# A 2:4 sparse linear layer on one core: SyncE loads x tile 5, tile 6 is transposed second, eight instead of fourteen short fillers, and other hand-written orders

## The chip, the core and the metric

The kernel runs on one core of one Trainium2 chip. The metric is the device time of one execution in microseconds, the median of several runs. TensorE is called PE in the profile, its weight loads PEld, VectorE DVE, ScalarE ACT, GpSimd POOL, SyncE SP.

## What is computed

```
wg  = w.reshape(256, 4, 1024)              # groups of four rows of w
mag = abs(wg)
thr = second largest of the four magnitudes
wp  = (wg * (mag >= thr)).reshape(1024, 1024)
out = einsum("bsd,df->bsf", x, wp) + b     # x: 16 x 512 x 1024, bf16
```

Each column of each group of four weights keeps its two largest. The pruned matrix then multiplies 8192 rows of x (64 tiles of 128 tokens), and the bias is added.

## The kernel before, in words

All 64 token tiles need 1024x1024 pruned weights, which don't exist at the start. The kernel therefore prunes the weights in six pieces (`pieces`, L137) and lets TensorE start on the first seven token tiles while later pieces are still being pruned. Pieces 0 to 3 are 256 columns each of the upper 512 rows, pieces 4 and 5 are 512 columns each of the lower 512 rows. A weight row of four neighbours lies on one partition ("packed"), so x must be transposed with the same grouping.

The start runs as follows. Loads: SyncE and ScalarE each issue half of weight piece 0 (L124, L125); then ScalarE issues x tile 5 and x tile 6 (L126, L127; upper half of the columns, 128 KB each), and SyncE tiles 3 and 4 together (L129, 256 KB), weight piece 1, tile 2, tiles 0 and 1, pieces 2, 3 and 4, and a transposing load of whole tiles (`load_lead`, L118). TensorE meanwhile runs fillers (L410, L411), matmuls of ones: six of 512 columns and fourteen of 128. After them four lists of tokens, written out by hand, set the order of each engine (L275 to L297); `run` (L400) emits them so that every token's forerunners (`needs`, L313) have been emitted, and the tile framework adds the semaphores. A list is the program order of its engine. The tokens are:

- `T5a`: TensorE transposes x tile 5 in four 128x128 steps (L203) into a PSUM bank; `C5a`: ScalarE copies it to SBUF (L208). Tiles in `LOOSE` (L196) use a bank of the larger PSUM pool, the others one of two banks, and then wait for the copy two transposes before.
- `abs hi lo t1 t2 thr mask mult` with a piece number: VectorE's pruning of that piece (L177, L166). For piece 0, `g` and `h` are rows 2 and 3 of each group in columns 0-127 and 128-255, `u` and `v` are rows 0 and 1 over all 256 columns; `x` and `y` are rows 0-1 and 2-3 of another piece. A token `abs3` in ScalarE's list is done by ScalarE (L169).
- `M5.0g`: TensorE's partial product of tile 5 with part g of piece 0 (L237). The partial products of pieces 0 to 3 for tiles 0 to 6 add up in PSUM banks (`psum_o`, six banks in rotation); `S3b0`, `U6h0`: ScalarE copies a full bank to SBUF (`stage`, L273), which frees it.
- `W0.0` and so on: SyncE (once ScalarE) re-spreads pruned weights into the natural row layout (`spread`, four DMAs); `Z`: loads of piece 5 and the bias; `X1`, `Y1`, `Y0`: transposing loads of x.
- `E`, `A`: first halves of later tiles in the natural layout (L251).

Behind the lists come the closes (second halves of tiles 0 to 11) and then seven batches of x tiles that TensorE multiplies with the full weights, 16 matmuls of 512 columns a tile. VectorE adds the bias and ScalarE issues the stores.

Of the kernel before, what the change touches and what calls it, by code (L numbers as in the profile page):

```python
# [10 lines left out]
def kernel(  # L11
# [62 lines left out]
    def pe(i):  # L74
        return seq("pe", i)
# [19 lines left out]
    def tokens(dram, t):  # L95
        a, b_ = next(s for s in GROUPS if s[0] <= t < s[1])
        return dram[a * P:b_ * P].rearrange("(p t) k -> p t k", p=P), t - a
    bias_sb = const.tile([P, Dout], bf16)

    def issue(eng, out_, in_):  # L100
        q = nc.sync if eng == "sp" else nc.scalar
        return seq(eng, q.dma_start(out_, in_))

    def load_w(g, c0, c1, ma=0, mb=4, eng="sp"):
        issue(eng, w_sb[:, g, ma:mb, c0:c1], wv[:, g, ma:mb, c0:c1])

    def load_x(ta, tb, eng="sp"):
        xs = const.tile([P, tb - ta, HK], bf16, name=f"x_{ta}")
        xv, n = tokens(xf, ta)
        issue(eng, xs[:], xv[:, n:n + tb - ta, :HK])  # L110
        for t in range(ta, tb):
            x_sb[t] = xs[:, t - ta, :]
# [10 lines left out]

    load_w(0, 0, 256, 0, 2)  # L124
    load_w(0, 0, 256, 2, 4, "act")  # L125
    load_x(5, 6, "act")  # L126
    load_x(SOLO, SOLO + 1, "act")  # L127
    act(nc.scalar.activation(spark[:], nc.const_aps.tensor(1.0, [P, 1], bf16), Act.Abs))
    load_x(3, 5)  # L129
# [13 lines left out]
    def filler(n, rep=1):  # L143
        for _ in range(n):
            pe(nc.tensor.matmul(warm_ps[:, :rep * P], lhsT=nc.const_aps.tensor(1.0, [P, P], bf16),  # L145
                                rhs=nc.const_aps.tensor(1.0, [P, rep * P], bf16), start=True, stop=True))
# [46 lines left out]
                self.tt(wp[:, self.g, ms, self.c0 + ca:self.c0 + cb], self.w[:, ms, ca:cb], self.mag[:, ms, ca:cb], Alu.mult)  # L193

    xpk = {}
    LOOSE = (4, 6)  # L196

    def transpose(t):
        xg = x_sb[t].rearrange("p (q m) -> p m q", m=4)
        bank = psum_o.tile([P, FH], fp32, name="ps") if t in LOOSE else psum_t.tile([P, FH], fp32, name="tp")  # L200
        tp = bank[:].bitcast(bf16)[:, :FH].rearrange("p (m q) -> p m q", m=4)
        for m in range(4):
            pe(nc.tensor.transpose(tp[:, m, :], xg[:, m, :], ident[:]))  # L203
        xpk[t] = tp
# [4 lines left out]
        xpk[t] = xt  # L209

    ps_open = {}
    SPLIT = {0: 6}
    part = {"": slice(0, 4), "x": slice(0, 2), "y": slice(2, 4), "a": slice(0, 2), "b": slice(2, 4)}
    part.update({c: slice(m, m + 1) for m, c in enumerate("uvst")})
    part.update({c: slice(2, 4) for c in "gh"})
    cols = {"g": (0, 128), "h": (128, 256), "j": (0, 128), "k": (128, 256)}
    half = {"a": slice(0, 1), "b": slice(1, 2)}
    pairs = [(3, 4), (SOLO, NPK), (0, 1), (2, 5)]
    pair_of = {t: q for q, pr in enumerate(pairs) for t in pr}
# [2 lines left out]
    def mm_piece(t, i, ms, cut=None):  # L222
# [8 lines left out]
        if new:  # L231
            ps_open[key] = psum_o.tile([P, FH], fp32, name="ps")
            left[key] = sum(SPLIT.get(a, 4) for a in ((0, 1) if t == SOLO and c0 < FH else (2, 3) if t == SOLO else (n, n)))
        ps = ps_open[key]
# [33 lines left out]
    def stage(key):  # L268
        solo = key[1] == "h"
        q, h, at = (pair_of[key[0]], key[2], int(key[0] != SOLO)) if solo else (key[0], key[1] // 2, key[1] % 2)  # L270
        if (q, h) not in staged:
# [2 lines left out]

    order = {  # L275
# [7 lines left out]
        ),  # L283
        "dve": (
# [4 lines left out]
        ),  # L289
        "act": (  # L290
            "C5a C3a C4a C6a C2a C0a C1a S3b0 S2b0 abs3 S0b0 U6h0 S3b1 S0b1 S2b1 S3b2 S0b2 S2b2 S2b3 S0b3 U6h1 "
            "S3b3 U7h0 W1.0q U7h1"
        ),
        "sp": (
            "W0.0 Z W0.1 X1 W1.0p Y1 W1.1 Y0"
# [1 line left out]
    }  # L297
    written = {"X0"}
    p = {}
    halves = {0: tuple("ghuv"), 1: ('x', 'y'), 2: ('u', 'v', 'y'), 3: ('x', 'y')}  # L300

    by_rows = {0}

    def all_of(tok, i):
        return [tok + x for x in halves.get(i, ("",))]

    def split_tok(tok):
        k = tok[-1] if tok[-1] in "xyabuvstghjk" else ""
        return (tok[:-1] if k else tok), k

    transposed = []

    def needs(eng, tok):  # L313
        base, k = split_tok(tok)
        if tok[0] == "C":
            return ["T" + tok[1:]]
        if tok[0] == "T":
            return ["C" + transposed[-2]] if int(tok[1:-1]) not in LOOSE and len(transposed) > 1 else []
        if tok[0] == "F":
            return []  # L320
        if tok[0] == "W":
            g, h = map(int, tok[1:4].split("."))
            return [n for i, pc in enumerate(pieces) if pc[0] == g and pc[1] // FH == h for n in all_of(f"mult{i}", i)]
        if tok[0] in "XYZ":
            return ["A0h1"] if tok == "Y1" else []
        if tok[0] == "A":
            return ["X0", f"W0.{tok.split('h')[1]}"] + ([f"U{NPK}h{tok[-1]}"] if tok[1] == "3" else [])
        if tok[0] == "E":
            return ["X0", f"W0.{tok[1]}"]
        if tok[0] == "U":  # L330
            t, h = map(int, tok[1:].split("h"))
            if t == NPK:
                return [f"E{h}"]
            return [f"M{t}.{x}" for i, pc in enumerate(pieces) if pc[0] == 0 and pc[1] // FH == h for x in all_of(str(i), i)]
        if base[0] == "M":
            t, i = base[1:].split(".")
            return [f"C{t}a", f"mult{i}{k}"]
        if tok[0] == "S":
            q, n = map(int, tok[1:].split("b"))
            return [f"M{t}.{x}" for i, pc in enumerate(pieces) if pc[0] == 0 and pc[1] // CW == n  # L340
                    for t in pairs[q] for x in all_of(str(i), i)]
        i, step = base[-1], base[:-1]
        before = {"abs": [], "hi": ["abs"], "lo": ["abs"], "t1": ["hi"], "t2": ["lo"],
                  "thr": ["t1", "t2"], "mask": ["thr", "hi", "lo"], "mult": ["mask"]}[step]
        out_ = []
        for b_ in before:
            if b_ in ("t1", "thr") and int(i) in SPLIT:
                out_ += [b_ + i + s for s in {"j": "j", "k": "k", "g": "j", "h": "k"}.get(k, "jk")]
            elif b_ == "t2":
                out_.append(b_ + i)  # L350
            elif b_ in ("abs", "hi", "lo") and int(i) in by_rows:
                out_ += [b_ + i + k] if step in ("hi", "lo") else [b_ + i + s for s in "ab"]
            else:
                out_.append(b_ + i + (k if b_ == "mask" else ""))
        return out_

    def emit(eng, tok):
        base, k = split_tok(tok)
        if tok[0] == "T":
            transpose(int(tok[1:-1]))  # L360
            if int(tok[1:-1]) not in LOOSE:
                transposed.append(tok[1:])
# [37 lines left out]
    def run(queues):  # L400
        while any(queues.values()):
            moved = False
            for eng, toks in queues.items():
                while toks and all(n in written for n in needs(eng, toks[0])):
                    emit(eng, toks[0])
                    written.add(toks.pop(0))
                    moved = True
            assert moved, queues

    filler(6, 4)  # L410
    filler(14)  # L411
    run({eng: order[eng].split() for eng in order})

    def load_nat(ta, tb):
# [120 lines left out]
```

## Time and profile before

| | us |
|---|---|
| median of 3 runs (232.63 to 233.07) | 232.82 |
| the profiled execution, its own time | 232.65 |
| its span, first to last instruction | 230.9 |
| PE busy | 227.4 |
| DVE busy | 107.8 |
| ACT busy | 13.3 |
| first filler starts | 0.78 |
| first transpose starts | 4.82 |
| first partial product starts | 6.07 |
| first matmul in the natural layout (E0) starts | 19.08 |

PE's busy time is modelled from pipelined matmuls: one of 128 columns is shown as 219 ns at full pace although the next one starts 56 ns later, so starts or the chain's rows tell the pace. In the timeline `x8` means eight instructions in one row, the first number is the start of the first, the second their busy time. A DMA's row has the time in which its engine issued it; when the data has landed is told by the rows of the issues.

### The profile page before, as it was taken

Reading aid. Unit: us, or ns where it says so; the run is one execution under the profiler, and the core shown is the slowest. Engines: PE = TensorE matmul, PEld = TensorE weight load, DVE = VectorE, ACT = ScalarE, POOL = GpSimd, SP = SyncE. Lnnn points to the kernel's source line nnn. Section 1 sums busy time; section 2 is a strip of 40 time slices with the busy share of each in tenths; the row PEclk is TensorE's granted clock in tenths of the full one; section 3 lists DMA queues with packets and bytes.
Section 4 is the critical chain, followed back from the end, with each engine's and each line's share of the span. In section 5 each row is a group of like instructions: output and inputs, shape, how many; then the busy total and the mean of one; then the engine's idle time right before and its main releaser. Section 6 shows DMA issues by size and latency. Waiting matters only on the chain.

```text
span 230.9 us, 2858 instructions
## 1 busy us (share of the span) xinstructions
PE 227.4 (99%) x1158; PEld 111.3 (48%) x1158; DVE 107.8 (47%) x196; ACT 13.3 (6%) x26; POOL 17.6 (8%) x15
## 2 busy tenths in 40 slices
PE   8999999999999999999999999999999999999995
PEld 5985444444444444444444444444444444444443
DVE  4999787744424424424424423423423433433434
ACT  3665100000000000000000000000000000000000
POOL 1000299700000000000000000000000000000000
PEclk9999999999999999999999999999999999999999
DMA  6999989995899322991159622796129932122122
GB/s 207 305 221 224 192 180 245 246 278 147 310 222 258 114 91 73 242 276 72 67 105 282 204 94 76 162 252 182 60 91 195 281 115 89 50 91 91 54 85 91
DMA packets 79292, 38.19 MB, mean 165 GB/s; under 512 B 64176, under 2 KB 71728, under 8 KB 79280
## 3 DMA queue, kind: packets, MB, share of 16 engines
q1 hardware_dynamic: 68352, 20.75, 44.9%
q10 hardware_dynamic: 10928, 17.27, 21.5%
q8 instruction: 9, 0.15, 0.3%
q14 instruction: 3, 0.02, 0.0%
HBM read 3.28 MB, written 16.78 MB: 87 GB/s over the span
## 4 chain that ended last, share of the span: by engine, by line
PE 99%; DVE 0%; issue 0%
PE ps L251 88%; PE ps L237 5%; PE tp L251 2%; PE ps L145 2%; PE tp L203 1%; PE ps L203 0%; DVE o L443 0%
## 5 line engine op out<-in xcount | busy, mean ns | idle before, releaser
L251 PE MATMUL ps<-wp_nat,xb 128*128 128x512 bf16 (+2 forms) x848 | 179.8, 375 | 0.0
L251 PEld LDWEIGHTS <-xb 128*128 128x128 bf16 x848 | 82.4, 98 | 97.5
L443 DVE TENSOR_TENSOR o<-ps,bias_sb 128x512 bf16<-128x512 f32 (+1 forms) x112 | 71.6, 677 | 113.8 <-PE ps L251 113.7
L439 POOL TENSOR_TENSOR st<-st,bias_sb 128x1024 f32<-128x1024 f32 x8 | 16.8, 2142 | 0.0
L251 PE MATMUL ps<-wp_nat,xlead 128*128 128x512 bf16 x64 | 14.8, 379 | 0.0
L251 PEld LDWEIGHTS <-xlead 128*128 128x128 bf16 x88 | 8.6, 98 | 10.2
L237 PE MATMUL ps<-wp,xt 128*128 128x256 bf16 (+1 forms) x126 | 13.0, 261 | 0.0
L445 DVE TENSOR_TENSOR o<-ps,st 128x512 bf16<-128x512 f32 x16 | 11.1, 692 | 2.8 <-PE ps L251 2.2
L237 PEld LDWEIGHTS <-xt 128*128 128x128 bf16 x126 | 11.1, 98 | 1.1
L251 PE MATMUL ps<-wp_nat,xlow 128*128 128x512 bf16 x48 | 10.7, 379 | 0.0
L273 ACT COPY st<-ps 128x512 f32<-128x512 f32 x14 | 7.4, 594 | 3.0 <-PE ps L237 3.0
L251 PEld LDWEIGHTS <-xlow 128*128 128x128 bf16 x48 | 5.0, 103 | 5.4
L166 DVE TENSOR_TENSOR wp<-w_sb,mag 128x256 bf16<-128x256 bf16 (+2 forms) x13 | 6.2, 483 | 0.1
L166 DVE TENSOR_TENSOR mag<-mag,hi 128x256 bf16<-128x256 bf16 (+2 forms) x13 | 6.0, 483 | 0.1
L251 PE MATMUL tp<-wp_nat,xlead 128*128 128x512 bf16 x24 | 6.0, 379 | 0.0
L145 PE MATMUL ps<-const-bfloat16-1.0 128*128 128x128 bf16 (+1 forms) x20 | 4.2, 408 | 0.8 <-PEq L519 0.8
L177 DVE TENSOR_SCALAR mag<-w_sb 128x512 uint16<-128x512 uint16 (+2 forms) x6 | 2.7, 468 | 3.3 <-DMA w_sb<-in_w_dram 3.3
L145 PEld LDWEIGHTS <-const-bfloat16-1.0 128*128 128x128 bf16 x20 | 2.3, 146 | 2.4 <-issue 2.4
L166 DVE TENSOR_TENSOR hi<-mag 128x512 bf16<-128x512 bf16 (+2 forms) x7 | 3.2, 458 | 0.0
L166 DVE TENSOR_TENSOR lo<-mag 128x512 bf16<-128x512 bf16 (+2 forms) x7 | 3.1, 458 | 0.0
L203 PEld LDWEIGHTS <-x 128*128 128x128 bf16 x28 | 2.2, 122 | 0.1
L428 POOL COPY pruned<-wp 128x1 bf16<-128x1 bf16 x1 | 0.2, 190 | 26.3 <-DVE wp L166 26.3
(18 smaller groups left out, 17.3 us busy)
## 6 DMA issues: line engine op xcount, KB each, us to landing
out_dram<-o ACTq DMA_DIRECT2D x58, 256.0 KB, 2.5
wp_nat<-wp SPq DMA_DIRECT2D x14, 128.0 KB, 3.6
out_dram<-o ACTq DMA_DIRECT2D x10, 128.0 KB, 1.7
w_sb<-in_w_dram SPq DMA_DIRECT2D x2, 512.0 KB, 4.7
w_sb<-in_w_dram SPq DMA_DIRECT2D x3, 256.0 KB, 4.6
x<-in_x_dram SPq DMA_DIRECT2D x2, 256.0 KB, 3.9
x<-in_x_dram ACTq DMA_DIRECT2D x2, 128.0 KB, 3.6
bias_sb<-in_b_dram SPq DMA_DIRECT2D x1, 256.0 KB, 4.5
```

The lines of the kernel that those rows point to most:

```text
L145: pe(nc.tensor.matmul(warm_ps[:, :rep * P], lhsT=nc.const_aps.tensor(1.0, [P, P], bf16), rhs=nc.const_aps.tensor(1.0, [P, rep * P], bf16), ...
L166: dve(nc.vector.tensor_tensor(out, a, b_, op=op))
L177: dve(nc.vector.tensor_single_scalar(self.mag[:, ms, :].bitcast(u16), self.w[:, ms, :].bitcast(u16), 0x7FFF, op=Alu.bitwise_and))
L203: pe(nc.tensor.transpose(tp[:, m, :], xg[:, m, :], ident[:]))
L237: pe(nc.tensor.matmul(ps[:, c0 + ca + d:c0 + cb + d], lhsT=xpk[t][:, m, :], rhs=wp[:, g, m, c0 + ca:c0 + cb], start=(new and m == ms.start ...
L251: pe(nc.tensor.matmul(ps, lhsT=xt[:, kt - koff, :], rhs=wp_nat[:, kt, c0:c1], start=(kt == first), stop=(kt == last)))
L273: act(nc.scalar.copy(staged[(q, h)][:, at, :, :].rearrange("p t c -> p (t c)"), ps_open.pop(key)[:]))
L428: pool(nc.gpsimd.tensor_copy(out=pruned[:], in_=wp[:, 1, 3, Dout - 1:]))
L439: pool(nc.gpsimd.tensor_tensor(st[:], st[:], bias.to_broadcast([P, 2, 2, CW]), op=Alu.add))
L443: dve(nc.vector.tensor_tensor(o[:, c0:c1], ps, bias_sb[:, c0:c1], op=Alu.add))
L445: dve(nc.vector.tensor_tensor(o[:, c0:c1].rearrange("p (n c) -> p n c", n=2), ps.rearrange("p (n c) -> p n c", n=2), add, op=Alu.add))
```

## The change

- SyncE loads tile 5, second in its queue, ahead of tiles 3 and 4; ScalarE loads only tile 6.
- The transposes go 5, 6, 4, 3, 2, 1, 0 in place of 5, 3, 4, 6, 2, 0, 1. Tile 6 uses the smaller PSUM pool (`LOOSE`).
- Eight short fillers instead of fourteen. The six long ones stay.
- Piece 0 is masked and multiplied in four parts of two rows by 128 columns (`e f g h`), and each tile takes eight matmuls of 128 columns for it (before, four of 128 and two of 256). Piece 2 is split in two parts instead of three.
- Abs of piece 2 moves from VectorE to ScalarE.
- The lists of TensorE, VectorE and ScalarE are in another order. SyncE's list is the same.

```diff
-    load_x(5, 6, "act")
+    load_x(5, 6)
     load_x(SOLO, SOLO + 1, "act")
     act(nc.scalar.activation(spark[:], nc.const_aps.tensor(1.0, [P, 1], bf16), Act.Abs))
     load_x(3, 5)
...
-    LOOSE = (4, 6)
+    LOOSE = (4,)
...
-    SPLIT = {0: 6}
+    SPLIT = {0: 8}
...
+    part.update({c: slice(0, 2) for c in "ef"})
-    cols = {"g": (0, 128), "h": (128, 256), "j": (0, 128), "k": (128, 256)}
+    cols = {"e": (0, 128), "f": (128, 256), "g": (0, 128), "h": (128, 256), "j": (0, 128), "k": (128, 256)}
...
         "pe": (
-            "T5a T3a T4a T6a M5.0g M3.0g M5.0h M3.0h M4.0g M4.0h T2a M6.0h M3.0u M6.0u M5.0u T0a M4.0u T1a "
-            "M2.0h M2.0g M2.0u M6.0g M0.0u M0.0h M0.0g M1.0g M0.0v M2.0v M1.0v M5.0v M6.0v M3.0v M4.0v M1.0u "
-            "M1.0h M2.1y M3.1y M5.1y M2.1x M6.1y M0.1x M1.1x M4.1x M6.1x M5.1x M0.1y M4.1y M3.1x M1.1y M2.2y "
-            "M3.2y M1.2y M6.2y M4.2y M4.2v M5.2y M5.2v M1.2v M2.2u M0.2v M0.2y M4.2u M0.2u M5.2u M6.2v M2.2v "
-            "M3.2u M1.2u M6.3x M0.3x M5.3x M3.2v M3.3x M1.3y M4.3y M1.3x M0.3y M4.3x M3.3y M6.3y M6.2u M2.3y "
-            "M2.3x M5.3y E0 A0h0 A2h0 A1h0 A3h0 E1 A2h1 A0h1 A1h1 A3h1"
+            "T5a T6a T4a T3a M5.0g M6.0g M6.0f M5.0f M4.0g M4.0f M3.0f M3.0g M4.0h M6.0h M5.0h T2a M4.0e M3.0h "
+            "M3.0e M5.0e T1a M6.0e T0a M2.0h M2.0g M2.0f M2.0e M1.0f M1.0e M1.0g M0.0e M0.0g M0.0f M0.0h M1.0h "
+            "M3.1x M4.1x M6.1x M5.1x M1.1y M6.1y M4.1y M0.1x M3.1y M1.1x M2.1x M5.1y M2.1y M0.1y M4.2x M0.2x "
+            "M5.2x M2.2x M1.2x M6.2x M1.2y M3.2y M3.2x M4.2y M0.2y M5.2y M6.2y M2.2y M6.3x M2.3x M0.3x M5.3x "
+            "M2.3y M5.3y M4.3x M4.3y M3.3y M3.3x M0.3y M1.3y M1.3x M6.3y E0 A0h0 A2h0 A1h0 A3h0 E1 A2h1 A0h1 A1h1 "
+            "A3h1"
         ),
         "dve": (
-            "abs0a abs0b hi0a lo0a lo0b hi0b t20 t10j t10k thr0j thr0k mask0g mask0h mult0g mult0h mask0u abs1 "
-            "mult0u hi1 lo1 t11 t21 mask0v thr1 mult0v mask1y mask1x mult1y abs2 mult1x lo2 hi2 t22 t12 thr2 "
-            "mask2y mask2v mult2y mask2u mult2v hi3 lo3 t13 t23 mult2u thr3 mask3x mult3x mask3y mult3y abs4 hi4 "
-            "lo4 t24 t14 thr4 mask4 mult4 abs5 lo5 hi5 t25 t15 thr5 mask5 mult5"
+            "abs0a abs0b hi0a hi0b lo0a lo0b t10j t20 t10k thr0j thr0k mask0g mask0f mult0g mult0f mask0h mask0e "
+            "mult0h abs1 mult0e lo1 hi1 t21 t11 thr1 mask1x mult1x mask1y mult1y lo2 hi2 t22 t12 thr2 mask2x "
+            "mult2x mask2y hi3 mult2y lo3 t13 t23 thr3 mask3x mult3x mask3y mult3y abs4 hi4 lo4 t24 t14 thr4 "
+            "mask4 mult4 abs5 lo5 hi5 t25 t15 thr5 mask5 mult5"
         ),
         "act": (
-            "C5a C3a C4a C6a C2a C0a C1a S3b0 S2b0 abs3 S0b0 U6h0 S3b1 S0b1 S2b1 S3b2 S0b2 S2b2 S2b3 S0b3 U6h1 "
-            "S3b3 U7h0 W1.0q U7h1"
+            "C5a C6a C4a C3a C2a C1a C0a abs2 S3b0 abs3 U6h0 S0b0 S2b0 S0b1 S3b1 S2b1 S0b2 S3b2 S3b3 S2b2 S0b3 "
+            "S2b3 U6h1 U7h0 W1.0q U7h1"
         ),
...
-    halves = {0: tuple("ghuv"), 1: ('x', 'y'), 2: ('u', 'v', 'y'), 3: ('x', 'y')}
+    halves = {0: tuple("efgh"), 1: ('x', 'y'), 2: ('x', 'y'), 3: ('x', 'y')}
...
     filler(6, 4)
-    filler(14)
+    filler(8)
```

The remaining lines let the helpers know the parts `e` and `f`, and make piece 5's abs come behind token `Z` in the emission.

More of the change, by code (lines that the diff above doesn't have):

```diff
@@ L307, in split_tok @@
     def split_tok(tok):
-        k = tok[-1] if tok[-1] in "xyabuvstghjk" else ""
+        k = tok[-1] if tok[-1] in "xyabuvstefghjk" else ""
         return (tok[:-1] if k else tok), k
@@ L342, in needs @@
         i, step = base[-1], base[:-1]
-        before = {"abs": [], "hi": ["abs"], "lo": ["abs"], "t1": ["hi"], "t2": ["lo"],
+        before = {"abs": ["Z"] if i == "5" else [], "hi": ["abs"], "lo": ["abs"], "t1": ["hi"], "t2": ["lo"],
                   "thr": ["t1", "t2"], "mask": ["thr", "hi", "lo"], "mult": ["mask"]}[step]
@@ L346, in needs @@
         for b_ in before:
-            if b_ in ("t1", "thr") and int(i) in SPLIT:
-                out_ += [b_ + i + s for s in {"j": "j", "k": "k", "g": "j", "h": "k"}.get(k, "jk")]
+            if b_ == "Z":
+                out_.append(b_)
+            elif b_ in ("t1", "thr") and int(i) in SPLIT:
+                out_ += [b_ + i + s for s in {"j": "j", "k": "k", "e": "j", "f": "k", "g": "j", "h": "k"}.get(k, "jk")]
             elif b_ == "t2":
```

## Prediction

> **What bounds the kernel now.** I read the page's first section, then the chain of waits in order of time, then the timeline of the first 20 us. The page says that TensorE is busy nearly all the time and that the chain that ends last is almost purely TensorE:
>
> ```profile
> PE 227.4 (99%) x1158; PEld 111.3 (48%) x1158; DVE 107.8 (47%) x196; ACT 13.3 (6%) x26; POOL 17.6 (8%) x15
> ...
> PE 99%; DVE 0%; issue 0%
> ```
>
> So time can only be won by starting TensorE's useful work earlier, by giving it less to do, or by letting it do the same at a higher clock. A stall of VectorE, ScalarE or a DMA counts only if it reaches TensorE. The chain of waits in order of time (start, length, line, count; a row begins where the one before it ends) shows where the useful work starts:
>
> ```profile
> 0.78 4.21 PE ps L145 x20
> 4.99 0.80 PE tp L203 x8
> 5.79 0.45 PE ps L203 x8
> 6.24 0.75 PE ps L237 x12
> ...
> 8.20 11.04 PE ps L237 x108
> 19.25 0.86 PE tp L251 x4
> ...
> 39.10 189.12 PE ps L251 x892
> ```
>
> Three things are read here. The first 4.2 us are fillers (L145). The first eight transposes take 0.80/8 = 100 ns each and the next eight 0.45/8 = 56 ns: TensorE runs at half pace until about 5.6 us and at full pace afterwards (the granted-clock column of a table by stretches says 1.00 throughout, since its records begin only near 5.6 us; the pace is what tells). And from 6.2 us on there is no hole: 14x0.056 + 94x0.109 = 11.0 us explains the row of 108 matmuls, and in the last row, where the last tile has 32 short matmuls in place of 16 full ones, 876x0.216 = 189.2 us explains 189.12. In starts instead of ends, T5 begins at 4.82 and the first partial product M5.0g at 6.07 us (timeline).
>
> What releases the first work, from the timeline, the issue rows and their landings:
>
> ```profile
> 1.27 0.97 ACTq L102 DMA_DIRECT2D x<-in_x_dram  x2
> ...
> 5.48 0.72 ACT L208 COPY xt<-tp 128x256 f32<-128x256 f32 x2 [1.71 <-PE tp L203]
> ...
> 5.67 0.49 DVE L166 TENSOR_TENSOR wp<-w_sb,mag 128x256 bf16<-128x256 bf16 x2
> ...
> x<-in_x_dram ACTq DMA_DIRECT2D x1, 128.0 KB, 3.5
> ```
>
> Tile 5 is issued at 1.27 us and lands 3.5 us later, at 4.78: exactly where the fillers end. The first pruned weights (mult0g) end at 5.67+0.29 = 5.96, so M5.0g can't start before about 6.00 even if its tile is ready.
>
> **The change, step by step**, against the profiled execution (232.65 us, of which the span is 230.9; the median of the three runs is 232.82, 0.17 above it).
>
> 1. **Six fillers fewer.** The 14 short fillers stand 107 ns apart (3.29 to 4.79 us). Eight end at 3.29+8x0.107 = 4.14. By itself this wins nothing; T5 must have its tile.
>
> 2. **Tile 5 by SyncE.** It is issued at 1.24 as before, now second in SyncE's queue and with 256 KB fewer ahead. Landing: below, the first SyncE load (128 KB) took 2.5 us, so 3.8; above, this tile's own row, 3.5 us, so 4.78. I take 4.3: the queue's second transfer halves from 256 KB (landed 4.80) to 128 KB, at some 300 GB/s worth 0.4 us. Tile 6 takes tile 5's old slot on ScalarE, so 4.78. Tiles 3 and 4 are issued at 1.75 instead of 1.24; with their own 3.6 us they land at 5.35 (bounds: 2.5 us, so 4.25; 4.4 us like the 256 KB weight load issued at 1.75, so 6.18). T5 runs 4.30 to 4.73, T6 4.78 to 5.21, T4 from 5.35, T3 to 5.90 if the pace doubles at 5.6 as now. M5.0g then waits for mult0g, 6.00 instead of 6.07: **-0.07**.
>
> 3. **The other loads of SyncE** are each issued some 0.5 us later. Even if every landing moves by all of that, its user comes later: x tile 2 at 7.1 for T2 at 7.2; tiles 0 and 1 at 7.8 for T1 at 7.9; weight pieces 1, 2, 3 at 6.7, 8.7, 9.6 for their abs at 6.7, 9.0, 9.9; the first transposed load (L118, 14.3 now) and the spread of the upper half (16.4 now), both at most 0.5 later, for E0 at 19.0. The second spread finds SyncE free at 16.1 rather than 15.6, when its last weights come (16.1), lands by 21.9, and E1 asks at 23.3; the second L118 load lands at 25.2 for a use at 27.7. All hidden; if the narrowest (tiles 0 and 1) missed, it would cost its excess, 0.1 or so.
>
> 4. **First products.** The order begins M5.0g M6.0g M6.0f M5.0f. Now TensorE stands 0.07 us at M3.0g, since tile 3's copy ends at 6.20 and TensorE sees it at 6.25, and 0.01 more after it. In the new order tile 6's copy ends near 5.8 and tile 4's near 6.2 for a use at 6.46; mult0f ends at 6.16 for a use at 6.23. **-0.08**, with a new wait of up to 0.03 inside the bounds.
>
> 5. **Piece 0 in eight matmuls of 128 columns** instead of four of 128 and two of 256: 8x0.056 - (4x0.056 + 2x0.109) = 0.006 us for each of seven tiles: **+0.04** (nothing at half pace, where 256 columns take twice as long as 128).
>
> 6. **Abs of piece 2 on ScalarE; piece 2 in two halves.** VectorE loses an abs (0.34) and two short steps (0.12) and waits about 0.15 for ScalarE's abs (1.06 us, starts near 9.0). mult2x ends near 12.3 and its first user M4.2x stands at 12.9: hidden. ScalarE's abs now stands ahead of S3b0, and M1.1y waits for the bank that S3b0 empties: S3b0 ends near 10.5 to 10.6, M1.1y's turn is 10.7. Cover of 0.1; if it is gone, the cost is about 0.1. I take 0.
>
> 7. **Everything behind** (W, X, Y, Z, the closes) keeps its order, and VectorE ends a little earlier; TensorE's rows from 19.25 on are a solid block. I take 0.
>
> Sum at this clock: -0.07 - 0.08 + 0.04 = **-0.11**, so 232.54.
>
> If the pace doubles later than 5.6, the saving is larger: at half pace throughout, the 16 transposes now end at 4.82+16x0.107 = 6.53, and in the new kernel at 5.35+8x0.107 = 6.21, which is -0.32 (steps 4 and 5 then vanish). The runs spread from 232.63 to 233.07; a clock released 0.8 us later costs 0.4 us of half-pace work, so I read the spread so, without proof. The profiled run is then one of the early ones, and the median run is 0.17 lower by a saving between 0.11 and 0.32: 232.82 - 0.22 = **232.6 us**.
>
> **The clock as a rival.** Today TensorE has no standstill over 0.05 us before the pace doubles, 4.8 us after the first matmul. The new kernel leaves it empty from 4.14 to 4.30, 4.73 to 4.78, 5.21 to 5.35 and 5.90 to 6.00, 0.45 us in all. If a standstill starts that count anew at 4.3, the doubling comes at 9.1; from 6.0 to 9.1 half the work is done, a loss of 1.55 us: 232.65 + 1.55 - 0.1 = **234.1 us**, slower by 0.6%. It decides from the point where such a gap matters at all; if the gaps only add to the count, it is +0.2 on top of the forecast. For it: the fillers are there to keep TensorE busy and six are gone. Against it: the pace doubled in the middle of transposes, and of the 4.8 us before it only 0.35 become empty. The Trainium skill ("TensorE: Matmul & The Clock Gate", Part 1) says that the clock is released after a free-running window of about 3.4 us in which the engine was busy; a window missed would put the release at 9.0 and the time at 234.05. Its Part 4 adds that transposes don't count as busy in the same way; then the new kernel has only 2.0 us of counted work in the window that ends at 5.6, against 2.6 now. The trace agrees that a window with 0.8 us of transposes passed, and can't show where the limit lies. Chance 0.18.
>
> **Other rivals.** *Tiles 3 and 4 land late* (6.18, as the weight load of the same size and issue time does): T4 and T3 end at 6.63, and M5.0g stands behind them: +0.56 - 0.04 = about **233.15 us**, on the edge of what can be told. For it: the same queue place; against it: 256 KB less lie ahead of them than lay ahead of that weight load. Chance 0.08. *Both early*: tile 5 lands by 4.14, tiles 3 and 4 near 5.1 and the old kernel's typical clock is late: T's end at 6.0 instead of 6.53, **232.3 us**. For it: the spread of the runs; against it: it needs low ends of two landings. Chance 0.12. *It changes nothing*: tile 5 lands at 4.78 as now; T's end at 6.07, only step 4 is left, 232.6 to 232.8; it lies inside the forecast.
>
> **How the numbers follow.** The forecast, 232.4 to 232.9, has 0.62. 0.2% is 0.47 us, about what a measurement of this kernel can tell from no change: faster means under 232.35, slower over 233.29. Faster: 0.12. Slower: 0.18 for the clock and half of the late landing, 0.22. Same: 0.66. The range goes from 232.3 to 233.5: it takes in the forecast, the late landing, and a release that comes up to 1.6 us later in the typical run; the full clock rival is left out.
>
> **What would show it.** Right: T5 at 4.2 to 4.5 right after eight fillers, T4 before 5.5, M5.0g at 6.0, no hole up to E0, and E0 at about 18.95 (19.08 now). Wrong: transposes and first products 107 ns apart beyond 7 us (clock); T4 at 6 us (landing); a gap before M1.1y (ScalarE's abs), or before T1, E0, E1 or the closes (SyncE's queue).

## The result and the profile after

| | before | after |
|---|---|---|
| median of 20 runs | 232.81 (232.53 to 234.38) | 233.25 (232.84 to 235.24) |
| ratio, 95% interval | | 1.0033, 1.0017 to 1.0050 |
| the profiled execution / its span | 232.65 / 230.9 | 232.99 / 231.2 |
| T5 starts | 4.82 | 4.07 |
| M5.0g starts | 6.07 | 6.42 |
| E0 starts | 19.08 | 19.41 |

The change makes the kernel slower by 0.33% over all runs; the medians alone are 0.44 us apart (0.19%), since the long runs hardly move the median of 20. The 20 runs lie in two groups: 14 from 232.84 to 233.61, with a median of 233.07, and six from 234.85 to 235.24 (before, one run of 20 was long, 234.38). So there are two losses to explain: 0.26 us in most runs, and another 2 us in some.

The profiled execution belongs to the first group. The chain of waits in order of time now begins with a DMA, where it began with fillers:

```profile
1.75 4.15 DMA x<-in_x_dram
5.90 0.05 issue
5.95 0.41 PE ps L203 x4
6.36 0.22 PE tp L203 x4
6.58 1.25 PE ps L238 x22
...
9.06 10.51 PE ps L238 x108
```

That first row is the load of tiles 3 and 4, from its issue to its landing. Its issue rows, first before (issued at 1.24, second in SyncE's queue), then after (issued at 1.75, third), with KB and us to landing:

```profile
x<-in_x_dram SPq DMA_DIRECT2D x1, 256.0 KB, 3.6
x<-in_x_dram SPq DMA_DIRECT2D x1, 256.0 KB, 4.2
```

The matmul timeline of the same stretch (in square brackets: idle time before the row, and what ended it):

```profile
4.07 0.76 PE L203 MATMUL tp<-ident,x 128*128 128x128 bf16 x8
5.95 0.41 PE L203 MATMUL ps<-ident,x 128*128 128x128 bf16 x4 [1.12 <-DMA x<-in_x_dram]
6.20 0.39 PE L203 MATMUL tp<-ident,x 128*128 128x128 bf16 x4
6.42 1.08 PE L238 MATMUL ps<-wp,xt 128*128 128x128 bf16 x16
```

T5 comes 0.75 us earlier than before and T6 right behind it, at full pace (here the pace doubled at 3.4 us, inside the fillers). Then TensorE waits until 5.9 for tiles 3 and 4, and everything behind stands 0.35 later. From M5.0g to E0 it takes 12.99 us (13.01 before), and from E0 to the end the same 209.1. From the page, the busy line and the chain's shares by engine: a DMA has 2% of the chain, and PE has lost 3.

```profile
PE 225.5 (98%) x1146; PEld 110.3 (48%) x1166; DVE 107.9 (47%) x193; ACT 14.2 (6%) x27; POOL 17.6 (8%) x15
...
PE 96%; DMA 2%; issue 1%; SPq 0%; DVE 0%
```

### The profile page after: what moved, and what is told of

The parts are those of the page before. It is cut to its first block, busy times and chain, and to the rows that moved or that the text cites. A ratio compares the mean times of both kernels' runs of the same rounds, so it can differ in the third digit from the quotient of the medians.

```text
span 231.2 us, 2853 instructions
## 1 busy us (share of the span) xinstructions
PE 225.5 (98%) x1146; PEld 110.3 (48%) x1166; DVE 107.9 (47%) x193; ACT 14.2 (6%) x27; POOL 17.6 (8%) x15
## 4 chain that ended last, share of the span: by engine, by line
PE 96%; DMA 2%; issue 1%; SPq 0%; DVE 0%
PE ps L252 88%; PE ps L238 5%; PE tp L252 2%; DMA x<-in_x_dram 2%; SPq L102 0%; PE tp L203 0%; PE ps L203 0%; DVE o L446 0%
## 5 line engine op out<-in xcount | busy, mean ns | idle before, releaser
L252 PE MATMUL ps<-wp_nat,xb 128*128 128x512 bf16 (+1 forms) x831 | 178.9, 375 | 0.9
L166 DVE TENSOR_TENSOR wp<-w_sb,mag 128x512 bf16<-128x512 bf16 (+2 forms) x12 | 6.1, 512 | 0.2
L166 DVE TENSOR_TENSOR mag<-mag,hi 128x512 bf16<-128x512 bf16 (+2 forms) x12 | 6.0, 511 | 0.2
L145 PE MATMUL ps<-const-bfloat16-1.0 128*128 128x128 bf16 (+1 forms) x14 | 3.2, 402 | 0.8 <-PEq L522 0.8
L145 PEld LDWEIGHTS <-const-bfloat16-1.0 128*128 128x128 bf16 x14 | 1.4, 125 | 2.4 <-issue 2.4
L208 ACT COPY xt<-tp 128x256 f32<-128x256 f32 x6 | 2.2, 374 | 2.6 <-PE tp L203 2.6
```

The source lines that it names most:

```text
L166: dve(nc.vector.tensor_tensor(out, a, b_, op=op))
L208: act(nc.scalar.copy(xt[:].bitcast(fp32), xpk[t].bitcast(fp32)))
L252: pe(nc.tensor.matmul(ps, lhsT=xt[:, kt - koff, :], rhs=wp_nat[:, kt, c0:c1], start=(kt == first), stop=(kt == last)))
```

## Theories

**Landing**: tiles 3 and 4, third on SyncE, land near 5.8, and T4 waits. **Clock**: holes before the pace doubles let some runs stay at half pace for another period; the loss is half of the time from M5.0g to the doubling. Rivals: the number of fillers alone, the new orders, the longer SyncE queue. The medians of the kernel before were 232.85 (e1 to e4), 233.14 (e5 to e8), 232.86 (e9 to e12), 232.91 (e13, e14) and 233.10 (e15, e16), each group on one chip, so ratios are what to compare. In the sections below, "level" is where most runs of a kernel lie, and a "long" run is one of those that stand 1 to 2.5 us above it.

## Which part of the change costs

**e2: fewer fillers alone** (in the kernel before).

```diff
-    filler(14)
+    filler(8)
```

> The kernel before with eight short fillers and nothing else changed: tile 5 lands at 4.78 as ever, so TensorE stands empty from 4.14 to 4.8 at half pace (from 3.8 or so if the pace doubles early). Landing theory: most runs at 232.7 to 232.9, as before. Clock theory: a hole of 0.65 is half of the new kernel's; some runs near 234.5 to 235, fewer than a third. Rival (the fillers' number alone counts): a third of the runs near 235.

Ratio 0.9996 (0.9985 to 1.0007); 232.54 to 233.42 in 12 runs. Eight fillers alone cost nothing that shows, and no run is long; a hole of 0.8 us is let pass here.

**e9: the orders alone** (the new kernel with old loads and fourteen fillers).

```diff
-    load_x(5, 6)
+    load_x(5, 6, "act")
...
-    filler(8)
+    filler(14)
```

> The new orders and splits with the old loads and the old fourteen fillers: what is left of the change is the orders alone. Window theory (in a fixed grid of 3.4 us the clock rises after a stretch filled by at least some three quarters): fillers to 4.8, one hole of 0.3 before T6, so no run above 234.5. Landing theory (the level of most runs of the new kernel comes from tiles 3 and 4 alone): M5.0g at 6.2 to 6.3, limited by tile 6 near 5.5, and a median within 0.2 above that of the kernel before. Rival (the new orders cost by themselves): a median 0.3 or more above it.

Ratio 1.0001 (0.9990 to 1.0012), the median 0.14 above, no long run. The orders are neutral in the median; in the profile (233.13) M5.0g came at 6.48, later than the 6.2 to 6.3 expected.

**e10: the load alone** (in the kernel before).

```diff
-    load_x(5, 6, "act")
+    load_x(5, 6)
```

> The kernel before with the load change alone: tile 5 second on SyncE, tiles 3 and 4 third; old orders, fourteen fillers. Landing theory: T3 stands second in the old order and waits for 5.6 to 5.9; M5.0g near 6.5 to 6.6 instead of 6.1 and a median 0.3 to 0.5 above the kernel before. Window theory: the hole is 0.4 to 0.7, so no run or one above 234.5. Rival (the later landing is hidden by mult0g, which ends at 6.0 anyway): within 0.1 of the kernel before.

Ratio 1.0027 (1.0018 to 1.0036), 232.98 to 233.84. The load change by itself slows the kernel, and that rules out that mult0g hides it. M5.0g came at 6.86 in its profile, later still than expected. Its chain of waits:

```profile
1.74 4.14 DMA x<-in_x_dram
5.88 0.05 issue
5.93 0.61 PE tp L203 x4
6.54 0.49 PE ps L203 x8
7.03 0.71 PE ps L237 x12
7.74 0.04 issue
7.78 0.41 PE tp L203 x4
```

The first row is again tiles 3 and 4. The second "issue" row shows a loss that the profile of after has not: T2 stands 0.26 before 7.78, since tile 2 landed at 7.73.

**e1: the change with fourteen fillers.**

```diff
-    filler(8)
+    filler(14)
```

> The new kernel with fourteen short fillers again; all else as in the change. Landing theory (the level of most runs, 233.0 to 233.3, comes from tiles 3 and 4, which land at 5.9): the level stays at 233.0 to 233.3, since T4 waits for 5.9 whatever is ahead. Clock theory (the runs near 235.0, 6 of 20, come from TensorE standing empty after the fillers): TensorE is now filled up to about 4.8 at half pace, the hole before T4 shrinks, and runs near 235 become rare (0 or 1). Rival (the fillers have no part in it, the hole before T4 alone does it): runs near 235 stay at about a third.

Ratio 1.0023 (1.0010 to 1.0035), 233.14 to 234.16, median 233.51: no run near 235, as expected if the fillers keep the clock, while the landing stays late (T4 at 5.69). That the median is 0.44 above 233.07 was not expected. Its profiled run (233.79) shows one reason in the chain of waits:

```profile
25.03 4.00 DMA wp_nat<-wp
29.03 0.04 issue
29.08 2.53 PE ps L252 x11
```

The second half of the spread W1.0 landed at 29.03, after its use: two holes of 0.18 and 0.65 us. In the kernel before it landed at 26.7 for a use at 27.9; in after at 28.0 for a use at 28.3.

**e3: the change with the old loads.** The diff is the first half of e9's.

> The new kernel with the old loads (tile 5 on ScalarE again, ahead of tile 6; tiles 3 and 4 second on SyncE), eight fillers and the new orders. Landing theory: tiles 3 and 4 land at 4.8 and tile 6 at 5.5; T6 at 5.5, T4 and T3 right behind, M5.0g near 6.15 to 6.2 and the level 232.7 to 232.9, as before the change. If the new orders were to blame for the level, it stays at 233.0 to 233.3. Clock theory: the hole is 0.65 before T5 and up to 0.4 before T6; runs near 235 in a tenth to a third.

Ratio 1.0065 (1.0040 to 1.0090), 232.89 to 235.52 in 7 runs, five of them over 234.4. Expected was a tenth to a third: a miss that helped. The new order has T6 second, which here waits for 5.57, so there are two holes, 0.7 before T5 and 0.35 before T6. Its profile (234.76) runs at half pace until 9.06, and M5.0g comes at 6.88.

**e12: the change again.**

> The new kernel once more, unchanged, on the chip of these three. Level theory: two groups again, most runs 0.2 to 0.4 above the kernel before and about a third near 2 above it.

Ratio 1.0023 (1.0007 to 1.0039), 232.60 to 234.82. The level is confirmed. Only one of 12 runs is near 235, with two at 234, so the share of long runs is not a fixed third. T4 at 5.71, and T2 waits for tile 2 (7.81), which starts it 0.35 after the matmul before:

```profile
6.32 1.41 PE L238 MATMUL ps<-wp,xt 128*128 128x128 bf16 x22
7.86 0.41 PE L203 MATMUL tp<-ident,x 128*128 128x128 bf16 x4
```

## The clock

**e5: four short fillers in the kernel before.**

```diff
-    filler(14)
+    filler(4)
```

> The kernel before with four short fillers: TensorE stands empty from 3.72 to about 4.8, 1.1 us in one piece; with eight (0.8 in its profile) no run was slow. Limit theory (empty time of 0.8 in the microseconds before the doubling is let pass, about 1.0 is not; then the doubling comes near 9 in place of 6): at least a third, rather two thirds, of the runs at 233.9 to 235. Rival (the long runs of the new kernel have another cause than empty time): runs stay at 232.5 to 233.9, as with eight and fourteen.

Eight of 12 runs are from 233.92 to 234.50, the others at 232.75 to 233.42. Ratio 1.0022 (1.0002 to 1.0042). In this place a hole of 0.8 us (e2) brings no long run and one of 1.4 (from 3.7 to 5.1 in this profile) brings many. It isn't the longest hole that decides: e3's is 0.7, shorter than e2's. The chain of its profile (234.16) shows the pace:

```profile
8.27 0.43 PE tp L203 x4
8.70 0.45 PE ps L237 x5
9.15 0.22 PE tp L203 x4
```

Four transposes take 0.43 us up to 8.7 and 0.22 from 9.15. M5.0g came at 6.79 and the doubling at 8.6: half of 1.8 us is 0.9; from M5.0g to E0 it took 13.80 instead of 13.01.

**e4 and e6: fillers in the hole before T4** (twelve and six; the diff shows six).

```diff
-            "T5a T6a T4a T3a M5.0g M6.0g ...
+            "T5a T6a F6 T4a T3a M5.0g M6.0g ...
```

> The new kernel with twelve short fillers put between T6 and T4, in the hole from 4.7 to 5.9; they end at 5.4 at full pace and at 6.0 to 6.5 at half pace. Landing theory: the level of most runs stays at 233.0 to 233.3, or up to 0.2 higher where half-pace fillers overrun the landing. Clock theory: with the hole filled the runs near 235 go (0 or 1). Rival (the number of fillers ahead of T5 decides): a third of the runs stays near 235.

> The new kernel with six short fillers between T6 and T4. At half pace they end near 5.65 and no longer overrun the landing of tiles 3 and 4 near 5.8; empty time is at most 0.5. Limit theory: no run above 234.5, and the level of most runs that of the new kernel's shorter ones, 232.9 to 233.3. Rival: a third of the runs near 235.

Twelve: ratio 1.0033 (1.0019 to 1.0047), 232.90 to 234.50; the group near 235 is gone, but the spread is broad. That the fillers run past the landing at half pace and push T4 back would explain it, but is not shown: the profiled run had the full pace from 3.64 on. Six: ratio 1.0006 (0.9989 to 1.0024), 11 of 12 runs from 233.02 to 233.75 and one at 235.20, where none was expected. One version alone proves little, since e12, the change itself, has only one such run in 12. Taken together, one of 36 runs with a hole filled (e1, e4, e6) is near 235, against seven of 32 of the change (its 20 and e12), and with larger holes five of 7 are long in e3 and eight of 12 in e5. So empty time in the first microseconds makes runs long; the profiles below show how, and for the change itself it is inferred.

**A fixed grid.** Two profiles, e7 and e8 (below), show the clock rise, fall and rise again, each 3.41 us after the last. Stretches of e7 (length, busy time and count of PE, PEld, DVE, ACT, POOL, granted clock, DMA share, GB/s):

```profile
1.06:4.47 3.41, 3.41 (x18) 1.92 (x17) 1.12 (x6) 1.49 (x2) 0.24 (x1) 1.00 0.70 214
4.47:7.88 3.41, 1.51 (x26) 1.35 (x25) 2.52 (x14) 1.26 (x4) 0.00 (x0) 1.00 1.01 315
7.88:11.30 3.42, 3.42 (x36) 3.41 (x34) 3.28 (x11) 0.67 (x3) 0.00 (x0) 0.50 1.27 239
11.30:14.70 3.40, 3.40 (x47) 3.20 (x45) 1.84 (x7) 3.24 (x6) 0.00 (x0) 1.00 1.06 218
```

The 1.00 of the first row is no measurement, since the clock's records begin at 4.47; the matmuls there start 107 ns apart, at half pace. After a full stretch the clock is up, after one with a hole of 2.1 us it falls to 0.50, after the next full one it is up again. With this grid, each doubling can be put down to the stretch before it. "Filled" counts each matmul by its columns at its pace (107 ns for 128 at half pace, 53 at full), from the starts in the traces, over 3.41 us:

| kernel, stretch | filled | without transposes | after it |
|---|---|---|---|
| before, 2.17 to 5.58 | 99% | 77% | rises |
| after, 0.03 to 3.44 | 78% | 78% | rises |
| e10, 3.08 to 6.50 | 79% | 50% | rises |
| e2, 2.58 to 5.99 | 78% | 46% | rises |
| e5, 5.18 to 8.60 | 100% | 40% | rises |
| e3, 2.23 to 5.65 | 69% | 56% | stays at half |
| e10, -0.33 to 3.08 | 68% | 68% | stays at half |
| e5, 1.77 to 5.18 | 59% | 57% | stays at half |
| after, 3.44 to 6.86 | 50% | 24% | stays at full |
| e16 (below), 3.62 to 7.03 | 47% | 20% | stays at full |
| e7, 4.47 to 7.88 | 39% | 17% | falls |
| e8, 3.84 to 7.25 | 37% | 11% | falls |

One reading fits all rows, and no stretch of the other profiles goes against it: the clock rises after a stretch filled by some limit between 69% and 78%, transposes counted, and falls after one filled by less than a limit between 39% and 47%. The place of the grid against the start of the kernel differs from run to run, so the same holes hit some runs and not others. The Trainium skill ("TensorE: Matmul & The Clock Gate", Part 1) tells of free-running windows of about 3.4 us; the traces agree (3.41). Part 4 of that page of the Trainium skill says that transposes don't count as busy in the same way; the column without transposes orders the rows wrongly (40% rises, 68% doesn't), so here the measurement decides: they count. The limits are read from the profiles of these runs and were not tried one by one.

In after, T6 ends at 4.7 to 5.0 and T4 starts near 5.8: with the gap ahead of T6 that is up to 30% or more of a stretch. Of its six long runs two show a granted clock of 0.993, or 231x0.007x2 = 3.2 us at half pace after a rise (it fell again, as in e7); the other four show 1.000, as runs do in which it first rises late (the records begin with the rise). No profile of a long run of this very kernel was taken; that they follow e3 and e7 is inferred, not shown.

## Why tiles 3 and 4 land late

**e7, e8: fewer issues on SyncE.** e7 moves tile 2 to ScalarE, behind tile 6; e8 has tile 3 on SyncE, and tiles 4 and 2 on ScalarE.

```diff
 e7:
+    load_x(2, 3, "act")
     load_x(3, 5)
...
-    load_x(2, 3)
 e8:
+    load_x(4, 5, "act")
+    load_x(2, 3, "act")
-    load_x(3, 5)
+    load_x(3, 4)
...
-    load_x(2, 3)
```

> The new kernel with x tile 2 issued by ScalarE, third in its queue: SyncE has as many issues as before the change, so the spread W1.0 is issued near 22.8 again instead of 23.2 and lands well ahead of its use. Tiles 3 and 4 stay third on SyncE. Landing theory: M5.0g stays near 6.3 to 6.4 and the shorter runs at 232.9 to 233.3. Queue theory (the longer SyncE queue costs as much as tiles 3 and 4): the shorter runs fall to 232.6 to 232.9. Limit theory: the hole before T4 is there, so about a third of the runs stays near 235.

> The new kernel with the early loads in equal parts on both queues: SyncE half of weight piece 0, tile 5, tile 3; ScalarE the other half, tile 6, tile 4, tile 2. SyncE has as many issues as before the change. Landing theory: tiles 3 and 4 land at 5.2 to 5.4 instead of 5.9, T4 and T3 end by 5.8, M5.0g at 6.0 to 6.1, E0 at 19.0: 232.5 to 232.7 for the shorter runs, better than both kernels; the hole before T4 is 0.3 to 0.5, so no run near 235. Rival (it is the amount of bytes, not the place in a queue): they land at 5.8 as now and the level stays at 233.0.

Both are misses: ratios 1.0072 (1.0041 to 1.0102) and 1.0053 (1.0029 to 1.0078), 6 of 10 and 5 of 9 runs near 235 and above. A third load on ScalarE's queue at 1.78 goes with a later landing of SyncE's third: tiles 3 and 4 land at 6.77 in e7, and at 6.32 and 6.53 in e8. Equal parts on two queues are no cure. What the longer SyncE queue costs by itself stays open, as e7 changes both queues.

**e11: tiles 3 and 4 second, tile 5 third.** The order begins T6 T4 T3, and T5 comes behind M6.0f (the copies follow, and the banks are taken as in the new kernel).

```diff
-    load_x(5, 6)
...
     load_x(3, 5)
+    load_x(5, 6)
...
-            "T5a T6a T4a T3a M5.0g M6.0g M6.0f M5.0f M4.0g M4.0f M3.0f M3.0g M4.0h ...
+            "T6a T4a T3a M6.0g M6.0f T5a M4.0g M4.0f M3.0f M3.0g M5.0g M5.0f M4.0h ...
```

> The new kernel with tiles 3 and 4 second on SyncE again and tile 5 third; the transposes go 6, 4, 3, then M6.0g M6.0f, then 5, and M5 comes after M4 and M3; the banks are taken in the order of the new kernel. Landing theory: tile 6 lands near 4.3, tiles 3 and 4 near 4.9, tile 5 near 5.3, so T3 ends by 5.4 to 5.8 and M6.0g starts at 6.0: 0.1 below to 0.1 above the kernel before. Window theory: holes of 0.3 to 0.5 in all, no run above 234.5. Rival (any third load on SyncE lands near 5.8, whatever its size): T5 waits until 5.8 behind M6.0f, without a loss, since M6 fills the time up to it; the level is the same, so this tells only whether the place of tiles 3 and 4 is what counts.

Tiles 3 and 4 land at 4.95, so second place, with its earlier issue, is what makes them early; tile 5 lands third at 5.22. M6.0g starts at 6.11, no run is long. But the ratio is 1.0027 (1.0017 to 1.0036): E0 comes 13.47 after the first product, since T5 (0.22 us) and waits of 0.09 and 0.18 now stand between products. The forecast of a level like before failed.

**e13: a load of 512 bytes in second place** (in the kernel before; never read).

```diff
+    tiny = const.tile([P, 2], bf16)
+    issue("sp", tiny[:], xf[0:P, 0:2])
     load_x(3, 5)
```

> The kernel before with a load of 512 bytes (never read) put second on SyncE, ahead of tiles 3 and 4: the queue place and the issue time of the new kernel, without tile 5's 128 KB ahead. Place theory (issue half a microsecond later, landing as much later): tiles 3 and 4 land near 5.3; M5.0g at most 0.1 later, 0 to 0.2 above the kernel before. Bytes theory (what counts is the 128 KB ahead of them on their queue): they land at 4.8 to 5.0 and nothing changes. Rival (the third load of the queue lands near 5.8 in any case): the level of the load change alone, 0.5 or more above.

The rival wins: with hardly a byte in second place, tiles 3 and 4 land at 5.94, 4.2 us after their issue as in after (3.6 in second place), and T3 waits:

```profile
4.78 0.39 PE L205 MATMUL tp<-ident,x 128*128 128x128 bf16 x4
5.99 0.41 PE L205 MATMUL tp<-ident,x 128*128 128x128 bf16 x4 [0.83 <-DMA x<-in_x_dram]
```

Ratio 1.0039 (1.0022 to 1.0056), with one of 11 runs at 235.20. Against the kernel before, the place costs 1.1 us of landing for half a microsecond of issue, and it needs no 128 KB ahead. Two things are not separated. The small load has as many packets as tile 5 (128, of 4 bytes in place of 1 KB). And tile 5's bytes are still moved at the same time, by ScalarE's queue.

**e14: tiles 3 and 4 as two loads** (transposes and copies 5, 6, 3, 4; tile 3 in place of tile 4 in the larger PSUM pool).

```diff
-    load_x(3, 5)
+    load_x(3, 4)
+    load_x(4, 5)
```

> The new kernel with tiles 3 and 4 as two loads of 128 KB, third and fourth on SyncE, transposed in the order 5, 6, 3, 4. Size theory (a 256 KB load lands late because it is one load, all of whose 16 parts must be done): tile 3 lands near 5.2 and tile 4 near 5.7; T3 fills half of the hole, and runs 2 above become rare; the level stays, as T4 still comes at 5.7. Bytes theory: both land together near 5.8, and all stays as in the new kernel. The extra issue moves x tiles 2, 0 and 1 another 0.4 back, which costs up to that at T2.

They land at 4.93 and 5.25, and the start is what the prediction had drawn: four transposes in one piece from 4.14 on, and M5.0g at 5.97.

```profile
4.14 1.06 PE L204 MATMUL tp<-ident,x 128*128 128x128 bf16 x8
4.99 0.63 PE L204 MATMUL ps<-ident,x 128*128 128x128 bf16 x4
5.42 0.44 PE L204 MATMUL tp<-ident,x 128*128 128x128 bf16 x4
5.97 1.39 PE L239 MATMUL ps<-wp,xt 128*128 128x128 bf16 x22
7.52 0.41 PE L204 MATMUL tp<-ident,x 128*128 128x128 bf16 x4 [0.16 <-DMA x<-in_x_dram]
7.77 0.61 PE L239 MATMUL ps<-wp,xt 128*128 128x128 bf16 x8
8.77 0.41 PE L204 MATMUL tp<-ident,x 128*128 128x128 bf16 x4 [0.39 <-DMA x<-in_x_dram]
```

But tile 2 now lands at 7.47 and tiles 0 and 1 at 8.73: T2 and T1 start 0.38 and 0.61 after the matmul before them, where 0.06 is the pace. Ratio 1.0040 (1.0023 to 1.0057). The gain of the start is given back 2 us later, and runs of 234.80 and 234.98 are still there, though the hole before T4 is gone.

**e15, e16: the split, with the issue time given back.** Both keep e14's split; the diffs show what they add. e15 loads tiles 0 to 2 as one and moves T2 and T1 back; e16 has ScalarE load tile 2.

```diff
 e15:
-    load_x(2, 3)
-    load_x(0, 2)
+    load_x(0, 3)
 e16:
     act(nc.scalar.activation(spark[:], nc.const_aps.tensor(1.0, [P, 1], bf16), Act.Abs))
+    load_x(2, 3, "act")
...
-    load_x(2, 3)
```

> The new kernel with tiles 3 and 4 as two loads, third and fourth on SyncE, and tiles 2, 0 and 1 as one load, so that SyncE has as many issues as the new kernel; T2 and T1 stand after eight more matmuls of piece 0. Size theory: tiles 3 and 4 land at 4.9 and 5.25 as with the split alone, the four transposes run with hardly a hole from 4.1, M5.0g starts at 6.0, and no run is 2 above. The one load of 384 KB lands late by the same theory, near 7.8 to 8.5, and TensorE stands up to 0.7 before T2: 0.2 to 0.6 above the kernel before. If it lands by 7.6: 0.1 to 0.3 below.

> The new kernel with tiles 3 and 4 as two loads on SyncE and tile 2 issued by ScalarE only after its table load, near 3.3, so that it does not compete with the first loads from ScalarE's queue. Size theory: tiles 3 and 4 land near 4.9 and 5.3, tile 2 near 6.5 to 7.2, tiles 0 and 1 near 7.8; M5.0g at 6.0, holes of at most 0.3 before T2 and T1: 0.2 below to 0.1 above the kernel before, and no run 2 above. Rival (a third load on ScalarE's queue slows SyncE's third and fourth loads, as where tile 2 went there early): tiles 3 and 4 land at 5.8 or later and runs 2 above come back.

e15: ratio 1.0064 (1.0047 to 1.0080), 233.96 to 235.05 in 6 runs. Tiles 3 and 4 land at 5.37 and 5.76, 0.5 later than expected, and the load of 384 KB at 8.74; the waits at T0 to T2 cost 1.2 us. e16: ratio 1.0043 (1.0024 to 1.0062), three of 12 runs over 234.9. ScalarE issued tile 2 at 1.85 after all, and tiles 3 and 4 landed at 5.87 and 6.32: its rival holds: with a third load on ScalarE, SyncE's third and fourth land 0.9 and 1.1 later than in e14.

What stays open: why a third load that is issued 0.5 us later lands 1.1 us later. In all runs third place and the later issue go together. A load of 128 KB in second place isn't needed for it (e13), and two queues don't cure it (e8); two smaller loads do better in e14 (and a little in e15), but the runs don't tell why. The packets in the traces show one more difference. In second place (before, e2, e9) all 256 packets of tiles 3 and 4 had started by 4.25 us. In third place (after, e1, e10, e12) 137 to 177 had, and in the next microsecond SyncE's queue moved 166 to 335 packets of 512 bytes, which are weight piece 1's, issued behind them, and only 78 to 109 of 1 KB. So the load behind takes part of the queue before the one ahead is done. Whether that is what delays the landing is not shown, since no version moves weight piece 1 alone. No version here beats the kernel before; e2, e6 and e9 can't be told from it.

## Why the prediction was wrong, point by point

- *Step 1, fewer fillers win nothing by themselves*: right (e2). Together with the later T4 they seem to matter for the clock: six of 20 runs of the change are long, none of 12 with fourteen fillers (e1).
- *Step 2, the landing of tiles 3 and 4 at 5.35, M5.0g at 6.00, -0.07*: **this step failed.** Tile 5 (4.02) and tile 6 (4.36) came earlier than the 4.30 and 4.78 forecast; tiles 3 and 4 landed at 5.90, M5.0g came at 6.42, +0.35. Their own 3.6 us from issue to landing, carried over to a later place, was the error: it is 4.2 there (after and e13). The row of weight piece 1, of the same size and in third place, had 4.4; the prediction used it as a bound alone. Of the 0.35, some 0.25 are the landing: in this profile the first weights landed 0.16 later than before and mult0g ended at 6.12, so M5.0g could not have started before about 6.17. The rival "tiles 3 and 4 land late" had the mechanism and, with 233.15 us, nearly the level (233.07), but a chance of 0.08; its landing of 6.18 was too late by 0.28. The measured median, 233.25, lies inside the range given because the range also took in this rival, not because the forecast's path held: that is luck.
- *Step 3, the other loads hidden*: right in the profile of after, but without the margin claimed. T2 waits 0.3 in e10 and e12. The spread W1.0 was not in the list; its margin fell from 1.2 to 0.3 us, and e1 lost 0.8 there.
- *Steps 4 and 5, -0.08 and +0.04*: from M5.0g to E0 0.02 less than before, where 0.04 were forecast: right, with a wait of 0.02 for tile 3's copy left over.
- *Steps 6 and 7, nothing*: right for the profile of after, 209.1 us from E0 on in both.
- *The clock as a rival*: right that empty time ahead of the doubling can cost a stretch at half pace, but not that a standstill starts a count anew: the stretches lie on a fixed grid. Its price was too low (234.1 forecast; 234.85 to 235.24 measured, of which 0.26 are the later landing). It was treated as all or nothing; it is a share of the runs, 6 of 20 and 1 of 12, and so it moves the median by less than its price.
- *The larger saving at a late clock*, which lifted the sum from -0.11 to -0.22, rested on T4 at 5.35, too.

## What to carry to other kernels

When a load is moved one place back in an issuing queue, take its landing from a row at that place and size (here weight piece 1's), not from its own old row plus the issue time; here 0.5 us of issue became 1.1 us of landing, and the later loads and spreads lost most of their margin as well. Early work in front of a late input only moves the hole, and a hole ahead of the useful work can cost more than its length: in these traces the clock follows how full a fixed stretch was. Fillers should cover the wait wherever it is: taking six of them away was harmless until the wait grew elsewhere.

## What the runs showed of the hardware that was not expected

- TensorE's clock rises or falls at the ends of fixed stretches of 3.41 us: up after 78% filled, not after 69%; down after 39%, not after 47%. Transposes count.
- It can fall again after one hole of 2.1 us inside a stretch (e7), although matmuls run before and behind it.
- With a third load from ScalarE at 1.8 us, SyncE's third load lands 0.9 to 1.4 us later: 6.77 in e7 against 5.90 in after for 256 KB, 5.87 in e16 and 6.32 in e8 against 4.93 in e14 for 128 KB.
- Behind a load of 512 bytes (with ScalarE's third load in place) 256 KB land as late, at 5.94, as behind one of 128 KB (without it), at 5.90 (e13 and after).
- Packets of a load issued later on the same queue are moved while the earlier load still has packets left (after, from 4.25 us on).
